# K of the last four-head step loaded in front of V of the step before it, and its TensorE scores moved

## The chip, the core and the metric

The kernel runs on one core of a Trainium2 chip. The core has a matrix engine (TensorE, PE in the profile; its weight loads are PEld), a vector engine (DVE), a scalar engine (ACT), GpSimd (POOL) and a queue engine (SP) that issues nearly all of the transfers here. Data comes from the chip's main memory into a memory of 128 partitions; matmul results go into a small accumulator memory (PSUM). The metric is device microseconds (us) of one execution; smaller is better.

## The reference

A decode step for a batch of B = 2: one token each, attention over a cache of 8,192 positions for 32 heads of 128, then a gated MLP. Nearly all of the bytes are the K and V caches, 2 x 32 x 8192 x 128 bf16 each.

```python
q = (x @ wq).reshape(B, Sq, Hq, Dh).transpose(0, 2, 1, 3)     # x is layernormed
scores = jnp.einsum("bhqd,bhkd->bhqk", q, k) * (Dh ** -0.5)
p = softmax(scores, axis=-1)
o = jnp.einsum("bhqk,bhkd->bhqd", p, v)
h = x + o.transpose(0, 2, 1, 3).reshape(B, Sq, Hq * Dh) @ wo
gate = layernorm(h) @ W_gate;  gate = gate * (gate > 0)
out = h + (gate * (layernorm(h) @ W_up)) @ W_down
```

## The kernel before

The 64 pairs of batch and head are done in 15 steps of four heads (steps 0 to 14; Q = LASTQ = 14) and two steps of two heads (15 and 16, called p0 and p1). K or V of a four-head step is 8 MB and fills one of three buffers of 128 partitions x 32,768 bf16 (`bufs`); K or V of a two-head step is 4 MB, half a buffer. Within a partition a buffer is a row of 256 tiles of 128 columns, one tile per group of cache positions.

For each step:

- `scores_pe` (L301) computes the scores of the last `npe` tiles of K on TensorE. In chunks of eight tiles, TensorE transposes them (L324), ACT copies the transposes back over the tiles (L325), and TensorE multiplies them with q (`times_q`, L315). The row that results is copied into the first eight of the now unused tiles (L333), transposed again (L337) and copied into the score column `scol` (L346). `npe` is 32; at the end 64 in step 14, 16 in step 15 and 32 in step 16 (`NPE_END`).
- `products` (L354) and `scores` (L365 to L373) compute the other `nv` tiles' scores on DVE: a product with q in place, four folds that halve the width, a sum into `scol`, and the maximum of each partition, `pm`.
- `largest` (L380) spreads the maxima by a matmul, and `exponentials` takes the minimum of their negatives (`nm`, L385) and has ACT write exp of the scores to `pgq` (four heads) or `pgp` (two heads), with their sums (L390).
- `values` (L403) multiplies the exponentials with V on TensorE, 64 matmuls for a four-head step, and ACT copies the result (L408); `diagonals` (L415) picks out each head's part.

The program order is written out by hand, and each engine takes its instructions in that order. All big loads stand on SP's queue. A load into a buffer waits for the last reader of the bytes that it overwrites, and a reader waits for the load that stands before it in program order and writes the bytes that it reads. In the loop over steps 0 to 13 (L477 to L497), V of the next step is loaded after `scores`, into the buffer that held K, and K of the step after next is loaded after `values`, into the buffer that held V. Step i has K in buffer 2i mod 3 and V in buffer (2i + 1) mod 3: K13 in 2, V13 in 0, K14 in 1, V14 in 2. K of steps 15 and 16 go to the halves of buffer 0, V of step 15 to the lower half of buffer 1 and V of step 16 to the lower half of buffer 2, in four pieces.

The weights of the second part follow in the free halves: `wo` in the upper half of buffer 1 (L506, L509: 16, 8 and 4 heads and the last four; the loads of 16, 8 and 4 heads start at columns 0, 8,192 and 12,288 of that half), W_gate and W_up in the upper half of buffer 2 (L544), W_down at the start of buffer 0 (L549). In program order the loads of V of step 15 and of `wo` stand behind `scores` of step 14 and in front of its `largest` and `exponentials`.

After step 14's exponentials, its values are done in eight groups of eight matmuls (`some_values`, L522), put between the TensorE scores of steps 15 and 16. Then come the values of step 15 (L559), DVE's `scores` of step 16 (L560), the output projection (`attend_set`, `attend`), the values of step 16 in column form (L426) and the MLP.

Of the kernel before, what the change touches and what calls it, by code (L numbers as in the profile page):

```python
# [23 lines left out]
def kernel(  # L24
# [14 lines left out]
    P = nc.NUM_PARTITIONS  # L39
    B, Sq, D = A_x.shape  # L40
    _, Hkv, Sk, Dh = A_k_cache.shape
    Hq = A_wq.shape[1] // Dh
    F = B_W_gate.shape[1]
    KC = D // P
# [3 lines left out]
    f32 = mybir.dt.float32  # L48
# [4 lines left out]
    LASTQ = B * NQ - 2  # L53
    TILE = NH * Sk * Dh // P
    HALF = TILE // 2
    TPC = 8
    VG = 4


    NPE = 32  # L60
    NPE_END = {LASTQ: 64, LASTQ + 1: 16, LASTQ + 2: 32}
    QZ = 64


    SETS = [(0, 16, 0), (16, 8, 16), (24, 4, 24)]
# [5 lines left out]
    FC = 11  # L71
# [44 lines left out]
    qrow = bufs[2][0:B, HALF:HALF + Hq * Dh]  # L116
    xr = bufs[2][0:B, HALF + Hq * Dh:HALF + Hq * Dh + D]

    wo = bufs[1][:, HALF:TILE]
    wgu = bufs[2][:, HALF:HALF + 2 * KC * F].rearrange("p (k c f) -> p k c f", k=2, c=KC)  # L120
    wd_sb = bufs[0][:, 0:FC * D].rearrange("p (c n) -> p c n", c=FC)


    class Step:
        def __init__(self, i):
            self.i = i
            self.quad = i <= LASTQ
            if self.quad:
                self.b, self.g = divmod(i, NQ)
                self.nh, self.nt = NH, TILE // Dh  # L130
                self.kt, self.vt = bufs[2 * i % 3], bufs[(2 * i + 1) % 3]
                self.qr = qrep[:, i, :]
                self.pg, self.zc = pgq, zc[:, self.b, self.g, :]
            else:
                k = i - LASTQ - 1
                self.b, self.g, self.k = B - 1, NQ - 1, k
                self.nh, self.nt = 2, HALF // Dh
                self.kt = bufs[0][:, k * HALF:(k + 1) * HALF]
                self.vt = bufs[1 + k][:, 0:HALF]
                self.qr = qpair[:, k, :]  # L140
                self.pg, self.zc = pgp[:, k], zc[:, self.b, self.g, 2 * k:2 * k + 2]
            self.npe = NPE_END.get(i, NPE)
            self.nv = self.nt - self.npe
            self.hp = P // self.nh
# [5 lines left out]
    Q = LASTQ  # L150

    def load_tile(cache, s, dst, pieces=1):
        h = NH * s.g + (0 if s.quad else 2 * s.k)
        n = s.nt * Dh
        w = n // pieces
        for k in range(pieces):
            nc.sync.dma_start(
                out=dst[:, k * w:(k + 1) * w], in_=_dram(cache, (s.b * Hkv + h) * Sk * Dh + k * w, [[n, P], [1, w]]),
            )
# [19 lines left out]
    with tc.manual_schedule():  # L179
# [105 lines left out]
        def sums(i):  # L285

            _, _, n, z = heads(i)
            z_ps[i] = ps.tile([P, n], f32, tag="mx", name="z_ps")
            nc.tensor.matmul(out=z_ps[i], lhsT=ones, rhs=z, start=True, stop=True)

        def shares(i):
            rzs[i] = small.tile([P, heads(i)[2]], f32, tag="rz", name="rz", bufs=2)
            nc.vector.reciprocal(out=rzs[i], in_=z_ps[i])

        def normalise(i):
            b, h0, n, _ = heads(i)
            nc.vector.tensor_tensor(out=ocol[:, h0:h0 + n, b], in0=o_ps[i][:, 0:n], in1=rzs[i], op=ALU.mult)

        scols = {}

        def scores_pe(s, between=lambda: None):  # L301


            U = s.npe // 4
            nh, nv = s.nh, s.nv
            row_ps = ps.tile([nh * U, 4 * P], f32, tag="row")

            def times_q(c0):
                for k in range(0, TPC, 4):
                    u = (c0 + k) // 4  # L310
                    if s.quad:
                        z = qz[:, QZ - NH - NH * u:QZ - NH - NH * u + NH * U]
                    else:
                        z = qzp[:, s.k, 14 - 2 * u:14 - 2 * u + 2 * U]
                    nc.tensor.matmul(  # L315
                        out=row_ps, lhsT=z, rhs=s.kt[:, (nv + c0 + k) * Dh:(nv + c0 + k + 4) * Dh],
                        start=(u == 0), stop=(u == U - 1),
                    )

            for c0 in range(0, s.npe, TPC):  # L320
                t_ps = ps2.tile([P, TPC, P], bf16, tag="tp")
                for k in range(TPC):
                    t = nv + c0 + k
                    nc.tensor.transpose(t_ps[:, k, :], s.kt[:, t * Dh:(t + 1) * Dh], ident)  # L324
                nc.scalar.activation(  # L325
                    out=s.kt[:, (nv + c0) * Dh:(nv + c0 + TPC) * Dh], in_=t_ps.rearrange("p t s -> p (t s)"), func=ACT.Copy,
                )
                between()
                if c0:
                    times_q(c0 - TPC)  # L330
            times_q(s.npe - TPC)
            rows = s.kt[0:nh * U, nv * Dh:nv * Dh + 8 * P].bitcast(f32)
            nc.scalar.activation(out=rows, in_=row_ps, func=ACT.Copy)  # L333
            between()
            sc_ps = ps.tile([P, 4, U, nh], f32, tag="row", name="sc_ps")
            for t in range(4):
                nc.tensor.transpose(  # L337
                    sc_ps[:, t].rearrange("p u j -> p (u j)"), rows[:, t * P:(t + 1) * P], ident_f[0:nh * U, 0:nh * U],
                )
            if s.i <= Q + 1:  # L340
                scols[s.i] = small.tile([P, TILE // Dh], f32, tag="scol", name="scol")[:, 0:s.nt]
            else:
                scols[s.i] = small.tile([P, s.nt], f32, tag="scolp", name="scolp")
            for j in range(nh):
                r = s.rows(j)
                nc.scalar.activation(  # L346
                    out=scols[s.i][r, nv:s.nt].rearrange("p (u t) -> p t u", t=4), in_=sc_ps[r, :, :, j], func=ACT.Copy,
                )

        def products(s, t0=0, t1=None):  # L350

            n = (s.nv if t1 is None else t1) - t0
            kv = _free(s.kt, t0 * Dh, [[Dh, n], [1, Dh]])
            nc.vector.tensor_tensor(out=kv, in0=kv, in1=_free(s.qr, 0, [[0, n], [1, Dh]]), op=ALU.mult)  # L354
# [42 lines left out]
        def values(s, u0, u1):  # L397

            r = slice(32 * (s.g % 4), 32 * (s.g % 4) + s.nh * VG)
            if u0 == 0:  # L400
                pv_ps[s.i] = ps2.tile([P, VG * Dh], f32, tag="o", name="pv_ps")
            for u in range(u0, u1):
                nc.tensor.matmul(  # L403
                    out=pv_ps[s.i][r, :], lhsT=s.pg[:, u].rearrange("p j t -> p (j t)"),
                    rhs=s.vt[:, u * VG * Dh:(u + 1) * VG * Dh], start=(u == 0), stop=(u == s.nt // VG - 1),
                )
            if u1 == s.nt // VG:
                nc.scalar.activation(out=pv[r, :], in_=pv_ps[s.i][r, :], func=ACT.Copy)  # L408
# [60 lines left out]
                )  # L469

        place_q(steps[0])
        def close(i):
            sums(i)
            shares(i)
            normalise(i)

        for i in range(Q):  # L477
            s = steps[i]
            scores_pe(s)
            place_q(steps[i + 1])  # L480
            products(s)
            scores(s)
            load_tile(A_v_cache, steps[i + 1], steps[i + 1].vt)
            largest(s)
            exponentials(s)
            if i - 1 in groups:
                close(i - 1)
            if i == 12:
                lay_rows(0, spread(0))
            values(s, 0, s.nt // VG)  # L490
            if i in groups:
                diagonals(i)
            if i + 2 <= Q:
                load_tile(A_k_cache, steps[i + 2], steps[i + 2].kt)
            else:
                for t in steps[Q + 1:]:
                    load_tile(A_k_cache, t, t.kt)  # L497


        s, p0, p1 = steps[Q:]  # L500
        scores_pe(s)
        products(s)
        scores(s)
        load_tile(A_v_cache, p0, p0.vt)
# [17 lines left out]
        def some_values():  # L522
            values(s, done[0], done[0] + 8)
            done[0] += 8
# [3 lines left out]
        load_tile(A_v_cache, p1, p1.vt, pieces=4)  # L528
        scores(p0)

        def values_or_largest():
            if done[0] < s.nt // VG:
                some_values()
            else:
                largest(p0)

        scores_pe(p1, values_or_largest)
        products(p1, 0, p1.nv // 2)
        exponentials(p0)
        sps = spread(1)  # L540
        products(p1, p1.nv // 2)
        for w, src, n in ((0, B_W_gate, 1), (1, B_W_up, KC // 2)):
            for c in range(0, KC, n):
                nc.sync.dma_start(  # L544
                    out=wgu[:, w, c:c + n], in_=_dram(src, c * P * F, [[F, P], [P * F, n], [1, F]]),
                )
# [89 lines left out]
        y = small.tile([P, B, KC], bf16, tag="y")  # L636
        nc.vector.tensor_tensor(out=y, in0=d_ps.rearrange("p c b -> p b c"), in1=hc, op=ALU.add)

        yrow = bufs[0][0:B * KC, HALF:HALF + P]
        yT_ps = ps2.tile([B * KC, P], bf16, tag="o")  # L640
        nc.tensor.transpose(yT_ps, y.rearrange("p b c -> p (b c)"), ident)
        nc.vector.tensor_copy(yrow, yT_ps)
# [31 lines left out]
```

## Time and profile before

| | |
|---|---|
| time, median of 3 runs | 662.42 us (662.28 to 664.31) |
| time of the profiled execution | 662.86 us |
| its span | 661.1 us |
| DVE busy | 527.8 us (80%) |
| PE busy | 386.1 us (58%) |
| ACT busy | 150.5 us (23%) |
| data moved by DMA | 281.44 MB, mean 426 GB/s |

The span is the stretch that the profiler covers; all times inside it count from its start. Busy shares are averages over the whole span. The strip of 40 slices on the page shows how they are spread, one slice being about 16.5 us, and the timeline lists single instructions with start, duration, engine, line, operation and what is written from what. For SP a row is the issue of a transfer; "us to landing" in the list of issues is from the issue until the data is there.

### The profile page before, as it was taken

The numbers are of one execution on the slowest core, as the hardware profiler recorded it, in microseconds if no ns is written. First come the engines' busy times: TensorE is split into PE (matmuls) and PEld (weight loads), VectorE is DVE, ScalarE is ACT, GpSimd is POOL, SyncE is SP. The second block draws the span as 40 slices with busy tenths as digits, with TensorE's granted clock in tenths as the row PEclk, the third lists the DMA queues.
The fourth block names the chain that finished last, engine by engine and source line by source line (L and its number), as shares of the span: only waits on it lengthen the run. The fifth ranks groups of instructions, "written<-read, shape, count | busy, mean of one in ns | idle before, by whom it ended". The sixth has DMA issues, their size and how long they took to land.

```text
span 661.1 us, 5492 instructions
## 1 busy us (share of the span) xinstructions
PE 386.1 (58%) x2347; PEld 179.1 (27%) x2347; DVE 527.8 (80%) x193; ACT 150.5 (23%) x323; POOL 5.2 (1%) x25
## 2 busy tenths in 40 slices
PE   3540854819276481927548192763909476397986
PEld 1120321304133240412214141221403233143446
DVE  2299696969969697996969789596988969698971
ACT  1130131311213132121312202131210313116420
POOL 2000000000000000000000000000000000000000
PEclk9875795959669595966959597695957869598985
DMA  9999989999999999999999999999999999999995
GB/s 381 445 440 444 444 386 444 437 441 444 432 406 444 433 436 440 429 420 444 437 424 434 436 436 433 444 417 440 440 417 436 440 429 436 433 408 434 421 417 223
DMA packets 8460, 281.44 MB, mean 426 GB/s; under 512 B 882, under 2 KB 2036, under 8 KB 3316
## 3 DMA queue, kind: packets, MB, share of 16 engines
q1 hardware_dynamic: 8432, 281.09, 98.7%
q8 instruction: 18, 0.29, 0.2%
q14 instruction: 6, 0.05, 0.0%
q10 hardware_dynamic: 4, 0.00, 0.0%
HBM read 281.09 MB, written 0.00 MB: 425 GB/s over the span
## 4 chain that ended last, share of the span: by engine, by line
DVE 35%; DMA 31%; PE 28%; ACT 4%; issue 1%; DVEq 0%; ACTq 0%
DMA tile<-in_A_k_cache_dram 29%; PE pv_ps L403 21%; DVE tile L354 16%; DVE tile L365 16%; ACT pgq L390 3%; DVE scol L369 2%; DMA tile<-in_A_wq_dram 2%; PE q_ps L240 1%; PE t_ps L324 1%; PE mx_ps L380 1%; PE row_ps L315 1%; PE o_ps L426 1%; DVE pm L373 1%; PE o_ps L415 0%; PE att_ps L459 0%
## 5 line engine op out<-in xcount | busy, mean ns | idle before, releaser
L354 DVE TENSOR_TENSOR tile<-tile,qrep 128x28672 bf16<-128x28672 bf16 (+1 forms) x15 | 224.3, 14950 | 73.5 <-DMA tile<-in_A_k_cache_dram 73.5
L403 PE MATMUL pv_ps<-tile,pgq 128*16 128x512 bf16 x960 | 245.3, 422 | 37.6 <-ACT pgq L390 37.6
L365 DVE TENSOR_TENSOR tile<-tile 128x14336 bf16<-128x14336 bf16 (+7 forms) x68 | 231.7, 3408 | 2.2
L403 PEld LDWEIGHTS <-pgq 128*16 128x16 bf16 x960 | 92.2, 98 | 184.1 <-issue 51.1
L380 PE MATMUL mx_ps<-nscale,pm 128*128 128x128 f32 x34 | 12.6, 470 | 175.0 <-DVE pm L373 175.0
L325 ACT ACTIVATE tile<-t_ps 128x1024 bf16<-128x1024 bf16 x70 | 70.0, 1023 | 30.7 <-PE t_ps L324 29.2
L390 ACT ACTIVATE pgq<-scol,nm 32x256 bf16<-32x256 f32 x60 | 30.3, 505 | 175.9 <-DVE nm L385 174.8
L408 ACT ACTIVATE pv<-pv_ps 16x512 f32<-16x512 f32 (+1 forms) x16 | 9.4, 589 | 239.1 <-PE pv_ps L403 238.3
L380 PEld LDWEIGHTS mx_ps<-nscale,pm 128*128 128x128 f32 x34 | 7.9, 290 | 177.6 <-DVE pm L373 176.7
L315 PE MATMUL row_ps<-tile,qz 128*32 128x512 bf16 (+1 forms) x128 | 38.8, 384 | 17.8 <-ACT tile L325 17.5
L324 PE MATMUL t_ps<-ident,tile 128*128 128x128 bf16 x560 | 42.6, 226 | 7.2 <-DMA tile<-in_A_k_cache_dram 7.2
L324 PEld LDWEIGHTS <-tile 128*128 128x128 bf16 x560 | 33.3, 101 | 29.2 <-issue 21.9
L369 DVE TENSOR_REDUCE scol<-tile 128x224 f32<-128x1792 bf16 (+2 forms) x16 | 31.1, 1944 | 1.6
L315 PEld LDWEIGHTS <-qz 128*32 128x32 bf16 (+1 forms) x128 | 10.8, 95 | 28.5 <-issue 21.8
L385 DVE TENSOR_REDUCE nm<-mx_ps 128x4 f32<-128x128 f32 (+1 forms) x17 | 5.0, 292 | 15.6 <-PE mx_ps L380 15.6
L346 ACT ACTIVATE scol<-sc_ps 32x32 f32<-32x32 f32 (+2 forms) x62 | 13.7, 222 | 10.3 <-PE sc_ps L337 9.2
L354 DVE TENSOR_TENSOR tile<-tile,qpair 128x6144 bf16<-128x6144 bf16 (+1 forms) x3 | 14.3, 4776 | 0.9 <-DMA tile<-in_A_k_cache_dram 0.9
L240 PE MATMUL q_ps<-tile,xn 128*2 128x512 bf16 x32 | 9.8, 471 | 8.3 <-DMA tile<-in_A_wq_dram 8.3
L243 DVE CAST tile<-q_ps 2x512 bf16<-2x512 f32 x8 | 5.4, 678 | 11.2 <-PE q_ps L240 11.2
L337 PE MATMUL sc_ps<-ident_f,tile 32*128 32x32 f32 (+3 forms) x68 | 7.3, 225 | 11.9 <-ACT tile L333 11.9
L333 ACT ACTIVATE tile<-row_ps 32x512 f32<-32x512 f32 (+3 forms) x17 | 10.0, 587 | 12.0 <-PE row_ps L315 12.0
L390 ACT ACTIVATION_READ_ACCUMULATOR pgq<-scol,nm 32x1 f32 x60 | 11.0, 184 | 0.0
(115 smaller groups left out, 114.2 us busy)
## 6 DMA issues: line engine op xcount, KB each, us to landing
tile<-in_A_k_cache_dram SPq DMA_DIRECT2D x2, 4096.0 KB, 26.1
tile<-in_A_wq_dram SPq DMA_DIRECT2D x1, 4096.0 KB, 12.1
tile<-in_A_v_cache_dram SPq DMA_DIRECT2D x1, 4096.0 KB, 21.6
tile<-in_A_v_cache_dram SPq DMA_DIRECT2D x4, 1024.0 KB, 21.1
tile<-in_A_wo_dram SPq DMA_DIRECT2D x1, 2048.0 KB, 26.1
tile<-in_B_W_gate_dram SPq DMA_DIRECT2D x4, 344.0 KB, 13.9
tile<-in_B_W_up_dram SPq DMA_DIRECT2D x2, 688.0 KB
tile<-in_A_wo_dram SPq DMA_DIRECT2D x1, 1024.0 KB, 28.0
```

The costliest lines, as they stand in the source:

```text
L240: nc.tensor.matmul(out=q_ps, lhsT=xn[:, c, :], rhs=wq_sb[:, c, n0:n0 + 4 * Dh], start=(c == 0), stop=(c == KC - 1),)
L315: nc.tensor.matmul(out=row_ps, lhsT=z, rhs=s.kt[:, (nv + c0 + k) * Dh:(nv + c0 + k + 4) * Dh], start=(u == 0), stop=(u == U - 1),)
L324: nc.tensor.transpose(t_ps[:, k, :], s.kt[:, t * Dh:(t + 1) * Dh], ident)
L325: nc.scalar.activation(out=s.kt[:, (nv + c0) * Dh:(nv + c0 + TPC) * Dh], in_=t_ps.rearrange("p t s -> p (t s)"), func=ACT.Copy,)
L333: nc.scalar.activation(out=rows, in_=row_ps, func=ACT.Copy)
L346: nc.scalar.activation(out=scols[s.i][r, nv:s.nt].rearrange("p (u t) -> p t u", t=4), in_=sc_ps[r, :, :, j], func=ACT.Copy,)
L354: nc.vector.tensor_tensor(out=kv, in0=kv, in1=_free(s.qr, 0, [[0, n], [1, Dh]]), op=ALU.mult)
L365: nc.vector.tensor_tensor(out=lo, in0=lo, in1=_free(s.kt, half, [[Dh, s.nv], [1, half]]), op=ALU.add)
L369: nc.vector.tensor_reduce(out=scol[:, 0:s.nv], in_=_free(s.kt, 0, [[Dh, s.nv], [1, 8]]), axis=AXIS.X, op=ALU.add,)
L380: nc.tensor.matmul(out=mx[s.i], lhsT=_free(pms[s.i], 0, [[0, P]]), rhs=nscale, start=True, stop=True)
L390: nc.scalar.activation(out=s.pg[r, :, j, :], in_=scol[r, :].rearrange("p (u t) -> p u t", t=VG), func=ACT.Exp, scale=SCALE, bias=nm[r, j:j ...
L403: nc.tensor.matmul(out=pv_ps[s.i][r, :], lhsT=s.pg[:, u].rearrange("p j t -> p (j t)"), rhs=s.vt[:, u * VG * Dh:(u + 1) * VG * Dh], start= ...
```

## The change

K of step 14 is loaded after `scores` of step 12, where V of step 13 was loaded, and V of step 13 after `values` of step 12, where K of step 14 was. To fit, K14 goes to buffer 0 and V13 to buffer 1, and what follows them changes places too: K of steps 15 and 16 and W_down go to buffer 1, V of step 15 and `wo` to buffer 0. The load of K of step 15 is put after the first half of step 13's values; the load of K of step 16 stays behind them.

`scores_pe` of step 14 is moved up from behind the loop into step 13, in front of its `largest`. Since the score column of step 13 is then still in use, the score columns of steps 14 to 16 get another place: inside the K buffer of the step itself, behind the eight tiles of the row (tiles nv + 8 and on, two bf16 columns for each f32 score).

Fewer tiles are scored on TensorE: 48 instead of 64 in step 14 and 16 instead of 32 in step 16, so DVE has 16 more in each. The last group of step 14's values comes behind step 16's `products` in program order, and `largest` of step 15 behind the seventh group instead of the last.

```diff
-    NPE_END = {LASTQ: 64, LASTQ + 1: 16, LASTQ + 2: 32}
-    QZ = 64
+    NPE_END = {LASTQ: 48, LASTQ + 1: 16, LASTQ + 2: 16}
+    QZ = 48
...
-    wo = bufs[1][:, HALF:TILE]
+    wo = bufs[0][:, HALF:TILE]
...
-    wd_sb = bufs[0][:, 0:FC * D].rearrange("p (c n) -> p c n", c=FC)
+    wd_sb = bufs[1][:, 0:FC * D].rearrange("p (c n) -> p c n", c=FC)
...
-                self.kt, self.vt = bufs[2 * i % 3], bufs[(2 * i + 1) % 3]
+                self.kt = bufs[0 if i == LASTQ else 2 * i % 3]
+                self.vt = bufs[1 if i == LASTQ - 1 else (2 * i + 1) % 3]
...
-                self.kt = bufs[0][:, k * HALF:(k + 1) * HALF]
-                self.vt = bufs[1 + k][:, 0:HALF]
+                self.kt = bufs[1][:, k * HALF:(k + 1) * HALF]
+                self.vt = bufs[2 * k][:, 0:HALF]
...
-            if s.i <= Q + 1:
-                scols[s.i] = small.tile([P, TILE // Dh], f32, tag="scol", name="scol")[:, 0:s.nt]
+            if s.i < Q:
+                scols[s.i] = small.tile([P, s.nt], f32, tag="scol", name="scol")
             else:
-                scols[s.i] = small.tile([P, s.nt], f32, tag="scolp", name="scolp")
+                scols[s.i] = s.kt[:, (nv + 8) * Dh:(nv + 8) * Dh + 2 * s.nt].bitcast(f32)
...
         for i in range(Q):
             s = steps[i]
             scores_pe(s)
             place_q(steps[i + 1])
             products(s)
             scores(s)
-            load_tile(A_v_cache, steps[i + 1], steps[i + 1].vt)
+            if i == Q - 2:
+                load_tile(A_k_cache, steps[Q], steps[Q].kt)
+            else:
+                load_tile(A_v_cache, steps[i + 1], steps[i + 1].vt)
+            if i == Q - 1:
+                scores_pe(steps[Q])
             largest(s)
             exponentials(s)
...
-            values(s, 0, s.nt // VG)
+            half = s.nt // VG // 2
+            values(s, 0, half)
+            if i == Q - 1:
+                load_tile(A_k_cache, steps[Q + 1], steps[Q + 1].kt)
+            values(s, half, 2 * half)
             if i in groups:
                 diagonals(i)
-            if i + 2 <= Q:
+            if i + 2 < Q:
                 load_tile(A_k_cache, steps[i + 2], steps[i + 2].kt)
+            elif i == Q - 2:
+                load_tile(A_v_cache, steps[Q - 1], steps[Q - 1].vt)
             else:
-                for t in steps[Q + 1:]:
-                    load_tile(A_k_cache, t, t.kt)
+                load_tile(A_k_cache, steps[Q + 2], steps[Q + 2].kt)
 
         s, p0, p1 = steps[Q:]
-        scores_pe(s)
         products(s)
         scores(s)
         load_tile(A_v_cache, p0, p0.vt)
...
-        def values_or_largest():
-            if done[0] < s.nt // VG:
-                some_values()
-            else:
+        def values_then_largest():
+            some_values()
+            if done[0] == s.nt // VG - 8:
                 largest(p0)
 
-        scores_pe(p1, values_or_largest)
+        scores_pe(p1, values_then_largest)
         products(p1, 0, p1.nv // 2)
         exponentials(p0)
         sps = spread(1)
         products(p1, p1.nv // 2)
+        some_values()
```

More of the change, by code (lines that the diff above doesn't have):

```diff
@@ L297, in normalise, with close @@
             nc.vector.tensor_tensor(out=ocol[:, h0:h0 + n, b], in0=o_ps[i][:, 0:n], in1=rzs[i], op=ALU.mult)
+        def close(i):
+            sums(i)
+            shares(i)
+            normalise(i)
         scols = {}
@@ L471 @@
         place_q(steps[0])
[L472 to L475, printed above, removed]
         for i in range(Q):
@@ L637 @@
         nc.vector.tensor_tensor(out=y, in0=d_ps.rearrange("p c b -> p b c"), in1=hc, op=ALU.add)
-        yrow = bufs[0][0:B * KC, HALF:HALF + P]
+        yrow = bufs[1][0:B * KC, HALF:HALF + P]
         yT_ps = ps2.tile([B * KC, P], bf16, tag="o")
```

## The prediction

> **What bounds the kernel now.** Times inside an execution are us from the start of the span. I read the page's strip of 40 slices first, then its list of DMA issues, then the timeline and the windows from 530 on, then the built program's order with what each instruction waits for.
>
> ```profile
> DVE  2299696969969697996969789596988969698971
> DMA  9999989999999999999999999999999999999995
> q1 hardware_dynamic: 8432, 281.09, 98.7%
> tile<-in_A_wo_dram SPq DMA_DIRECT2D x1, 2048.0 KB, 26.1
> tile<-in_A_wo_dram SPq DMA_DIRECT2D x1, 1024.0 KB, 28.0
> ```
>
> The transfers run from the first slice into the last; DVE, next at 80%, has pauses. All loads are on one queue. The reader should keep the last line: the 1 MB load of wo's eight heads takes 28.0 us from issue to landing, because others are in front of it. Now the timeline around the scores of step 14:
>
> ```profile
> 589.24 12.74 DVE L365 TENSOR_TENSOR tile<-tile 128x12288 bf16<-128x12288 bf16 x4
> 603.94 0.42 DVE L373 TENSOR_REDUCE pm<-scol 128x1 f32<-128x256 f32 x1
> 604.24 1.38 SPq L506 DMA_DIRECT2D tile<-in_A_wo_dram  x3
> 604.94 0.29 DVE L385 TENSOR_REDUCE nm<-mx_ps 128x4 f32<-128x128 f32 x1 [0.58 <-PE mx_ps L380]
> 605.33 0.51 ACT L390 ACTIVATE pgq<-scol,nm 32x256 bf16<-32x256 f32 x1 [1.42 <-DVE nm L385]
> 607.84 3.58 PE L403 MATMUL pv_ps<-tile,pgq 128*16 128x512 bf16 x8 [0.61 <-ACT pgq L390]
> 611.45 18.82 SPq L157 DMA_DIRECT2D tile<-in_A_v_cache_dram  x4
> ```
>
> wo's loads go out at 604.2 to 605.2, just ahead of the exponentials of step 14 (605.33), on which TensorE's values (607.84) wait. The load of eight heads, second of the three at L506, is issued at about 604.8 and lands at 604.8 + 28.0 = 632.8. The end of the kernel:
>
> ```profile
> 627.33 0.49 PE L380 MATMUL mx_ps<-nscale,pm 128*128 128x128 f32 x2
> 628.47 3.35 DVE L354 TENSOR_TENSOR tile<-tile,qpair 128x6144 bf16<-128x6144 bf16 x1
> 631.86 3.36 DVE L365 TENSOR_TENSOR tile<-tile 128x6144 bf16<-128x6144 bf16 x1
> 639.68 0.29 DVE L373 TENSOR_REDUCE pm<-scolp 128x1 f32<-128x128 f32 x1
> 640.79 0.49 PE L380 MATMUL mx_ps<-nscale,pm 128*128 128x128 f32 x2
> ```
>
> From the largest score of step 16 (640.79) to the end (661.1) one thing follows another, 20.3 us. The last W_down load, issued at 648.7, lands 7.3 us later, at 656.0; the output is written from 659.04.
>
> **What the program's order adds.** After the change the score column of step 14 (scol) lies in its own K buffer, buffer 0, at 128-column tiles nv + 8 = 216 to 220. wo now lies in the upper half of that buffer, and its eight-head load writes 4,096 columns from 16,384 + 16 x 512 = 24,576, which are tiles 192 to 224. In program order this load stands in front of the exponentials of step 14, as before. The built program shows the result: the first of these exponentials waits for that load's completion count, which it did not before, and the load waits for DVE's pm, the reduction that reads scol. So the exponentials of step 14 start when the load has landed (and take its bytes as the scores, which does not alter their time).
>
> **The change, part by part.**
>
> Exchange of K14 and V13. Both are 8 MB and take each other's place: K14 goes out at 531.1 (V13's time) and lands where V13 did, 531.1 + 25.8 = 556.9; V13 at 551.7 + 24.6 = 576.3. Values of step 13 began at 573.90 and now wait for V13 until 576.3, 2.4 later, and end at 592.1 instead of 589.74. The loads that this releases, K of 15 and of 16, go out at 585.3 and 592.1 while V14 is in transfer (to about 595.6, 19.3 us for 8 MB after 576.3), so the queue stays full: 0 on the transfers. Without that cover it would be 2.4.
>
> TensorE scores of step 14: 48 tiles instead of 64, so 16 transposes, 4 row products and 2 evictions of 1.02 less; what remains runs from 559 to about 569, after the scores of step 13. TensorE is idle there (0.00 busy in 560 to 570) and the next largest begins at 570.17. It costs nothing there; two evictions too late would be 2, still inside the 2.4 above.
>
> DVE, step 14: products no longer wait 4.96 for K14 and start at 571.3. With 208 tiles instead of 192: products 12.96 x 208/192 = 14.04, folds 12.74 x 208/192 = 13.80, reduction 1.75 to 1.90, pm 0.42, gaps 0.2. pm ends at 601.6 instead of 604.36. That is the gain of 2.7 that the reordering offers.
>
> wo's loads follow pm's release and go out at about 602 instead of 604.2, behind the same bytes (K15, K16, V15: 4 MB each, then 2 MB of wo). The queue being full, they land as before: the eight heads at 632.8. The bound from below is the shortest landing in the trace, 7.3 after issue (128 KB of W_down), so not before 609, which only rival 3 comes near; from above, the last piece of wo, issued 605.7 + 29.7 = 635.4. I take 632.8, the same load in the same place.
>
> The wait: exponentials of step 14 at 632.9 instead of 605.33. Behind them ACT holds the evictions for the TensorE scores of 15 and 16 and the later exponentials. TensorE holds the values of 14 and all after; SP holds the four pieces of V16 (issued from 611.45 before), gate and up, which need the values to free buffer 2. DVE does products and folds of 15 but its reduction waits for TensorE's row products, since their score column is in K too.
>
> From there, in TensorE order with the durations of before: exponentials 2.5, values start at 635.4 (607.84 before: +27.5). The stretch up to the score transposes of step 15 is unchanged (607.84 to 616.06), so 643.6. Then eight values 1.8, eight transposes 0.55, eight values 1.8, transposes 0.55, eight values 1.8, a last row product 0.2, eight values 1.8: 652.1. The largest of 15 follows, 0.49: 652.6. Before it ended at 627.82, 20.0 after the values began; now 17.2, since step 16 has two chunks of transposes fewer (with their values blocks moved behind).
>
> DVE then: nm 0.3, the two spreads 0.5, second products of step 16 (56 tiles: 3.35 x 56/48 = 3.91): 657.3. From there to pm of 16 the old rows took 639.97 - 631.74 = 8.23 for 96 tiles; with 112, folds (3.36 + 3.34) and reduction 0.95 grow by a sixth, 1.1, to 9.35: pm ends at 666.7. TensorE does the remaining values of 14 (654.8), and the 32 of step 15 from 657.8 in 6.9 to 8.7, done at 664.7 to 666.5. So DVE ends last, and the largest of 16 begins at 666.7 instead of 640.79: +25.9.
>
> Loads after the stall: V16's first piece goes out at 639.0; the remaining 8.2 MB at about 420 GB/s need 19.5, and with 2.4 of start (12.1 less 9.7 for 4 MB at rate) they land by 662. Their users come at 652 + 26 = 678 and later. Nothing on the path.
>
> The last 20.3: the same instructions; none waits for a load any more, at most 0.5 less. A lower clock there could cost up to 2, but 64 matmuls of L426 took 1.81 at a granted 0.55 to 0.59 and 64 of L459 1.74 near 1.00, so I take 0.
>
> Sum: 661.1 + 25.9 = 687.0 span. Around the span lie 662.86 - 661.1 = 1.76, so the profiled execution would be 688.8; it stood 0.44 above the median 662.42, which gives 688.4.
>
> **A rule against the row.** Landing at 632.8 rests on the queue's order: the last five landings before were V15 625.5, wo 630.3, 632.8, 634.0 and 635.4, in order of issue and spaced by size (2, 1, 0.5, 0.5 MB). The Trainium skill, DMA: Bandwidth & Descriptors, section Queues, rings and completion order, says that a DMA engine takes turns between the queue rows that have work, at packet granularity, and takes one ring's descriptors in order. All loads here share one row, so the trace agrees with its second half; turns between transfers would make the third rival below.
>
> **Rivals.**
>
> 1. The words of the change hold and the exponentials aren't held (not slower). They would start at 602.5, but the transposes of step 15 stand in front of the values on TensorE and need K15, which DVE and TensorE got at 606.2 before: values start 0.8 earlier, no more. DVE is equal until 631.8 and then has 16 tiles more in step 16, +1.1, so pm ends at 641.1 and the largest of 16 begins 0.3 later; the last landing stays at 656.0. Span 661.4, time 662.7. It decides if the exponentials begin by 605.3. For it: the 4.96 wait and the TensorE work of 591 to 603 do go away. Against it: the wait stands in the program, on a load that can't be issued before pm. 6 in 100.
>
> 2. Faster by over 0.3% (under 660.4): W_down would have to land 2 us before 656.0, with a queue at 98.7% and the same bytes. 2 in 100.
>
> 3. Transfers of the queue share the engines. Then the 1 MB load, issued at 602.6 with four others unfinished, lands after 5 x 1.05 MB at 430 GB/s = 12.2, near 615; values at 617.5, largest of 15 at 634.7 instead of 652.6, 18 less: 670. The 28.0 row speaks against it. 2 in 100.
>
> 4. The stall costs more: TensorE, idle for 29 us, stays at half clock (0.50 in 605 to 610, values 0.43 each against 0.21). The 48 values after the first eight would add 48 x 0.21 = 10: 698. Against it: clock 0.82 in 610 to 615 and 1.00 after, following a cold start as well. 4 in 100.
>
> **How the numbers follow.** The forecast has 86 in 100. Its own uncertainty is the landing (632 to 635.4), the clock of the end (0 to 2) and the DVE sums (1): 684 to 693. Outside are rivals 1 to 4 and a tail of the forecast, below 2 in 10. About 0.3% (2 us) is what a measurement of this kernel tells from no change. Slower: 86 + 2 + 4 = 92; same 6; faster 2.
>
> **What would show it.** Right: exponentials of step 14 idle for some 30 us until a wo load lands, near 632.9; ACT and TensorE empty from about 607 to 633; a slice or more of low GB/s around 635 to 641; K14 products starting at 571.3 without a DMA wait; pm of 14 near 601.6; largest of 16 near 666.7 and 20 us from there to the end. Wrong: exponentials near 602.5, or a landing of that load well before 630.

## The result and the profile after

The changed kernel takes 686.08 us (median of 6 runs, 685.62 to 687.46) against 663.06 for the kernel before beside it: ratio 1.0348, 95% interval 1.0332 to 1.0364, 23.0 us slower. The profiled execution took 686.07, its span is 684.2. In this kernel the exponentials of step 14 run after a load of wo has written over their score column, so they take bytes of wo in place of the scores of step 14, and its heads don't get the weights of the reference. The time is the subject here; the repair is in the first two experiments.

The page of the changed kernel, the rows that answer to those of before:

```profile
DVE  2298796969699796969699795969889799972381
DMA  9999999999999999999999999999999999999670
GB/s 387 461 437 429 429 426 429 427 433 437 430 430 433 445 433 434 437 433 426 429 442 437 433 430 433 434 433 433 442 433 429 430 423 433 420 432 402 231 276 3
q1 hardware_dynamic: 8432, 281.09, 95.5%
tile<-in_A_wo_dram SPq DMA_DIRECT2D x1, 1024.0 KB, 31.5
```

Up to slice 37 the queue is as full as before. A slice is now 17.1 us: the hole is in slices 38 and 39 (231 and 276 GB/s, from 633 on), and the last slice has hardly a transfer. The transfers did not get slower; they were stopped. The timeline of the changed kernel (start, duration, engine, line, operation; in brackets the idle time before and what ended it) shows where:

```profile
570.79 14.02 DVE L360 TENSOR_TENSOR tile<-tile,qrep 128x26624 bf16<-128x26624 bf16 x1
576.15 16.08 PE L409 MATMUL pv_ps<-tile,pgq 128*16 128x512 bf16 x64 [5.60 <-DMA tile<-in_A_v_cache_dram]
600.67 0.42 DVE L379 TENSOR_REDUCE pm<-tile 128x1 f32<-128x256 f32 x1
600.97 1.39 SPq L516 DMA_DIRECT2D tile<-in_A_wo_dram  x3
633.03 0.51 ACT L396 ACTIVATE pgq<-tile,nm 32x256 bf16<-32x256 f32 x1 [40.17 <-DMA tile<-in_A_wo_dram]
635.54 3.33 PE L409 MATMUL pv_ps<-tile,pgq 128*16 128x512 bf16 x8 [29.36 <-ACT pgq L396]
638.90 6.59 SPq L158 DMA_DIRECT2D tile<-in_A_v_cache_dram  x4
641.36 1.09 DVE L375 TENSOR_REDUCE tile<-tile 128x112 f32<-128x896 bf16 x1 [20.65 <-PE row_ps L321]
656.60 3.89 DVE L371 TENSOR_TENSOR tile<-tile 128x7168 bf16<-128x7168 bf16 x1
665.63 0.29 DVE L379 TENSOR_REDUCE pm<-tile 128x1 f32<-128x128 f32 x1
666.06 0.46 PE L386 MATMUL mx_ps<-nscale,pm 128*128 128x128 f32 x2 [2.15 <-DVE pm L379]
```

ACT is idle for 40.17 us before the first exponential of step 14 and is released by a load of wo. Some 10 us of that are no loss: the scores of step 14 are now done early, and ACT would be idle until about 602.7 in any case (second experiment). The hold is the other 30.3. The eight-head load went out at 601.4 and landed 31.5 later, at 632.9. Behind the exponential TensorE waits 29.36, DVE 20.65 (its reduction of step 15), and SP's four pieces of V16 leave at 638.9 instead of 611.45. The first two rows are the exchange: the products of step 14 no longer wait for K14, and the values of step 13 wait for V13. The windows (us busy and, in brackets, instructions of PE, PEld, DVE, ACT and POOL; then TensorE clock, DMA share, GB/s) give the same by stretch:

```profile
600.00:633.00 33.00, 2.39 (x12) 1.77 (x12) 16.72 (x10) 0.00 (x0) 0.00 (x0) 0.50 0.98 415
634.00:641.00 7.00, 5.46 (x28) 2.12 (x29) 0.00 (x0) 3.48 (x8) 0.00 (x0) 0.68 0.16 46
641.00:661.00 20.00, 18.84 (x114) 8.82 (x110) 14.10 (x11) 5.74 (x14) 0.00 (x0) 1.00 1.02 397
```

TensorE does 2.39 us of work in 33, ACT none, while the queue still runs. When ACT is let go, the queue has emptied, at 46 GB/s; from 641 on the released loads fill it again.

### The profile page after: what moved, and what is told of

Same layout as the page of the kernel before. It is cut to its first block, busy times and chain, and to the rows that moved or that the text cites. A ratio compares the mean times of both kernels' runs of the same rounds, so it can differ in the third digit from the quotient of the medians.

```text
span 684.2 us, 5411 instructions
## 1 busy us (share of the span) xinstructions
PE 377.6 (55%) x2307; PEld 176.1 (26%) x2307; DVE 532.0 (78%) x193; ACT 146.1 (21%) x319; POOL 5.1 (1%) x25
## 4 chain that ended last, share of the span: by engine, by line
DVE 39%; DMA 35%; PE 21%; ACT 2%; issue 1%; SPq 0%; DVEq 0%; ACTq 0%
DMA tile<-in_A_k_cache_dram 28%; DVE tile L360 18%; DVE tile L371 18%; PE pv_ps L409 16%; DMA tile<-in_A_wo_dram 5%; ACT pgq L396 2%; DVE scol L375 2%; DMA tile<-in_A_wq_dram 2%; PE q_ps L241 1%; PE mx_ps L386 1%; PE o_ps L432 1%; DVE pm L379 0%; DVE tile L375 0%; PE att_ps L465 0%; DVE nm L391 0%
## 5 line engine op out<-in xcount | busy, mean ns | idle before, releaser
L409 PE MATMUL pv_ps<-tile,pgq 128*16 128x512 bf16 x960 | 241.5, 418 | 69.0 <-ACT pgq L396 63.4
L371 DVE TENSOR_TENSOR tile<-tile 128x14336 bf16<-128x14336 bf16 (+5 forms) x68 | 233.7, 3437 | 2.2
L331 ACT ACTIVATE tile<-t_ps 128x1024 bf16<-128x1024 bf16 x66 | 65.9, 1022 | 27.2 <-PE t_ps L330 25.8
L321 PE MATMUL row_ps<-tile,qz 128*32 128x512 bf16 (+1 forms) x124 | 38.2, 390 | 18.4 <-ACT tile L331 18.1
L330 PE MATMUL t_ps<-ident,tile 128*128 128x128 bf16 x528 | 40.3, 227 | 9.4 <-DMA tile<-in_A_k_cache_dram 9.4
L375 DVE TENSOR_REDUCE scol<-tile 128x224 f32<-128x1792 bf16 x14 | 28.3, 2020 | 1.4
L375 DVE TENSOR_REDUCE tile<-tile 128x112 f32<-128x896 bf16 (+1 forms) x3 | 4.1, 1352 | 20.9 <-PE row_ps L321 20.7
L360 DVE TENSOR_TENSOR tile<-tile,qpair 128x7168 bf16<-128x7168 bf16 (+1 forms) x3 | 15.4, 5130 | 2.8 <-DMA tile<-in_A_k_cache_dram 2.8
L352 ACT ACTIVATE scol<-sc_ps 32x32 f32<-32x32 f32 x56 | 12.2, 218 | 8.3 <-PE sc_ps L343 7.3
L343 PE MATMUL sc_ps<-ident_f,tile 32*128 32x32 f32 (+2 forms) x68 | 7.3, 225 | 11.1 <-ACT tile L339 11.1
L339 ACT ACTIVATE tile<-row_ps 32x512 f32<-32x512 f32 (+2 forms) x17 | 10.0, 586 | 13.0 <-PE row_ps L321 13.0
## 6 DMA issues: line engine op xcount, KB each, us to landing
tile<-in_A_wo_dram SPq DMA_DIRECT2D x1, 1024.0 KB, 31.5
```

What stands on the lines that cost most here:

```text
L321: nc.tensor.matmul(out=row_ps, lhsT=z, rhs=s.kt[:, (nv + c0 + k) * Dh:(nv + c0 + k + 4) * Dh], start=(u == 0), stop=(u == U - 1),)
L331: nc.scalar.activation(out=s.kt[:, (nv + c0) * Dh:(nv + c0 + TPC) * Dh], in_=t_ps.rearrange("p t s -> p (t s)"), func=ACT.Copy,)
L352: nc.scalar.activation(out=scols[s.i][r, nv:s.nt].rearrange("p (u t) -> p t u", t=4), in_=sc_ps[r, :, :, j], func=ACT.Copy,)
L371: nc.vector.tensor_tensor(out=lo, in0=lo, in1=_free(s.kt, half, [[Dh, s.nv], [1, half]]), op=ALU.add)
L375: nc.vector.tensor_reduce(out=scol[:, 0:s.nv], in_=_free(s.kt, 0, [[Dh, s.nv], [1, 8]]), axis=AXIS.X, op=ALU.add,)
L409: nc.tensor.matmul(out=pv_ps[s.i][r, :], lhsT=s.pg[:, u].rearrange("p j t -> p (j t)"), rhs=s.vt[:, u * VG * Dh:(u + 1) * VG * Dh], start= ...
```

## The experiments

Each run is compared with the kernel before on the same chip.

**Does taking the wait away give the 23 us back?** Two ways, so that neither's side effect decides. In the first the score column of step 14 leaves the K buffer, and its exponentials read the scores again:

```diff
-    ones = consts.tile([P, P], f32)
+    ones = consts.tile([P, 1], f32)
...
-            nc.tensor.matmul(out=z_ps[i], lhsT=ones, rhs=z, start=True, stop=True)
+            nc.tensor.matmul(out=z_ps[i], lhsT=_free(ones, 0, [[0, P]]), rhs=z, start=True, stop=True)
...
+            elif s.i == Q:
+                scols[s.i] = small.tile([P, s.nt], f32, tag="scolq", name="scolq")
...
```

> The changed kernel, but the score column of step 14 has a place of its own outside the K buffer, so no load of wo writes over it; to make room the tile of ones is one column, read with a step of zero. Theory (the wait on the wo load is the whole loss): exponentials of step 14 at about 602.5 instead of 633.0, values from about 607, time 662.7 (661 to 664.5), within 0.3% of before. Rival (the exchange of K14 and V13, the moved scores or DVE's 16 + 16 more tiles cost a part of the 23): the time stays above 665, by that part.

Measured: 662.39 us, ratio 0.9989 (0.9979 to 0.9998); the first exponential of step 14 starts at 602.26. In the second the column stays and the loads move:

```diff
+        largest(s)
+        exponentials(s)
         for k, (h0, n, at) in enumerate(SETS):
...
-        largest(s)
-        exponentials(s)
```

> The changed kernel with the score column where it is, but the four loads of wo behind the exponentials of step 14 in program order. Theory: the exponentials wait for DVE alone and start at about 602.5; the eight-head load waits for them instead, goes out at about 605 and lands at 633 as before, since the queue is full; time 662.7 (661 to 664.5), same as e1_own_column within 1 us. Rival (the place inside the K buffer itself costs, by waits of DVE or ACT on neighbouring bytes): slower than e1_own_column by more than 1.5 us.

Measured: 662.55 us, ratio 0.9982 (0.9970 to 0.9993). The timeline of this second kernel:

```profile
600.96 0.42 DVE L379 TENSOR_REDUCE pm<-tile 128x1 f32<-128x256 f32 x1
601.26 4.74 SPq L518 DMA_DIRECT2D tile<-in_A_wo_dram  x3
602.71 0.51 ACT L396 ACTIVATE pgq<-tile,nm 32x256 bf16<-32x256 f32 x1 [8.78 <-DVE nm L391]
605.61 7.62 DVE L360 TENSOR_TENSOR tile<-tile,qpair 128x14336 bf16<-128x14336 bf16 x1 [2.99 <-DMA tile<-in_A_k_cache_dram]
```

The exponential starts at 602.71, released by nm. The three loads now take SP 4.74 instead of 1.39, because the second waits for the exponentials; it costs nothing, as the queue in front of it is full. Both kernels lie within 0.2 us of each other. So the place inside the K buffer costs nothing by itself that these two runs could tell, and everything else in the change together is a gain of 0.1 to 0.2%: the rivals of both runs fall.

**Does the overlap alone, in the kernel before, make the loss?** Nothing exchanged, nothing moved; the exponentials of step 14 read the load's bytes:

```diff
-            if s.i <= Q + 1:
+            if s.i == Q:
+                scols[s.i] = s.kt[:, (nv + 8) * Dh:(nv + 8) * Dh + 2 * s.nt].bitcast(f32)
+            elif s.i <= Q + 1:
```

> The kernel before with one edit: the score column of step 14 lies inside its K buffer (tiles 200 to 204 of buffer 1), where the eight-head load of wo, which stands ahead in program order, writes; its exponentials read that load's bytes, as in the changed kernel. Nothing is exchanged or moved. Theory: exponentials at 632.9 instead of 605.3, largest of step 16 near 667.7, 18.1 to 20.3 from there to the end, time 686 to 690 (+23 to +27). Rival (the loss needs the exchange or the new order of TensorE's work): 663, no change.

Measured: 688.90 us, ratio 1.0387 (1.0369 to 1.0405), 25.3 us more than 663.64 beside it. Its timeline:

```profile
632.23 0.51 ACT L392 ACTIVATE pgq<-tile,nm 32x256 bf16<-32x256 f32 x1 [27.95 <-DMA tile<-in_A_wo_dram]
668.27 0.49 PE L382 MATMUL mx_ps<-nscale,pm 128*128 128x128 f32 x2
```

The releaser is the same load, and the exponential starts 0.8 us earlier than in the changed kernel; the largest of step 16 starts 0.6 us later than expected. The overlap is sufficient by itself.

**Does the time follow that one landing?** The eight-head load is put ahead of V of step 15; the exponentials still read its bytes:

```diff
+        h0, n, at = SETS[1]
+        nc.sync.dma_start(
+            out=wo[:, at * D:(at + n) * D], in_=_dram(A_wo, h0 * Dh * D, [[n * D, P], [1, n * D]]),
+        )
         load_tile(A_v_cache, p0, p0.vt)
-        for k, (h0, n, at) in enumerate(SETS):
+        for k, (h0, n, at) in enumerate(SETS[::2]):
```

> The changed kernel, with the eight-head load of wo issued ahead of V of step 15 instead of behind it and the sixteen-head load; the exponentials still read that load's bytes. Theory (the time follows that landing one to one): it lands 6 MB, 14.6 us, earlier, near 618.3 instead of 633.0, and the time is 686.1 - 14.6 = 671.5 (669.5 to 673.5). Rival (the stall is of another load, or of the queue as a whole): 686. A landing that moves while the time follows by less than half would mean that another chain takes over from there.

Measured: 671.52 us, ratio 1.0122 (1.0107 to 1.0137). The load landed at 617.7 (issued 601.5, 16.2 later):

```profile
617.74 0.51 ACT L396 ACTIVATE pgq<-tile,nm 32x256 bf16<-32x256 f32 x1 [24.37 <-DMA tile<-in_A_wo_dram]
651.78 0.46 PE L386 MATMUL mx_ps<-nscale,pm 128*128 128x128 f32 x2 [0.49 <-DVE pm L379]
```

The exponential is 15.3 earlier than in the changed kernel, the largest of step 16 14.3 earlier, the time 14.6 shorter. One to one within a microsecond; no other chain takes over down to this point. It also shows that the wait is for one load's place in the queue, not for the queue to drain.

**What is the rest of the change worth?** As the second experiment, with the old TensorE shares:

```diff
-    NPE_END = {LASTQ: 48, LASTQ + 1: 16, LASTQ + 2: 16}
-    QZ = 48
+    NPE_END = {LASTQ: 64, LASTQ + 1: 16, LASTQ + 2: 32}
+    QZ = 64
...
-            some_values()
-            if done[0] == s.nt // VG - 8:
+            if done[0] < s.nt // VG:
+                some_values()
+            else:
                 largest(p0)
...
-        some_values()
```

> As e2_loads_behind, but with the old TensorE shares (64, 16 and 32 tiles in steps 14, 15 and 16) and the old places of the last value group and of the largest of step 15; what stays of the change is the exchange of K14 and V13 and the scores of step 14 moved up. Theory: 662.2 (660.5 to 664): the last landing (near 656.0) sets the end, so the 1.1 us that DVE saves in step 16 against e2_loads_behind comes out as 0 to 1. Rival (DVE's 16 more tiles are the bound at the end): faster than e2_loads_behind by 1.2 us or more.

Measured: 661.45 us, ratio 0.9974 (0.9963 to 0.9986). It is 1.1 us under the second experiment by the medians, 0.5 by the ratios (0.0008 of 663), and the two intervals overlap: between theory and rival, so the times don't settle how much the DVE tiles cost. In the profiled executions, one of each kernel, the largest of step 16 begins at 639.31 here and at 640.93 in the second experiment, and the spans differ by the same 1.6 (659.6 and 661.2). In both, TensorE comes to it straight from the values of step 15, with pm done 0.7 and 0.6 before. Those values start 0.6 earlier here, because TensorE doesn't wait 1.74 for a reciprocal behind DVE's longer product, and they run 1.0 shorter (8.74 against 9.75). The trace of this run shows no wait for a load of W_down. So the theory's reason, that the last landing sets the end, isn't borne out, and the rival's DVE tiles act through TensorE's start; why the values run shorter wasn't tried. It is the fastest kernel of the study, 0.26% under the one before, which is less than the 0.3% named in the prediction.

## Why the prediction was right

The exchange: products of step 14 start at 570.79 (forecast 571.3), values of 13 at 576.15 (576.3), pm of 14 ends at 601.1 (601.6). Each of these moved as worked out, within 0.5, and the transfers stayed full up to 633.

The wait: landing at 632.9 (632.8), first exponential 633.03 (632.9), values from 635.54 (635.4), largest of 15 done at 652.0 (652.6), pm of 16 at 665.9 (666.7), largest of 16 at 666.06 (666.7). From 640.79 this is +25.3; the prediction had 25.9. The last transfer, issued at 655.5, landed 7.8 later, at 663.3 (662), nowhere on the path. The prediction had 8.2 MB of loads behind the stall. The list of issues adds up to 8,256 KB (V16 4,096, gate and up 1,376 each, W_down 1,408), which is 8.45 MB at 1,024 bytes a KB, so at its 420 GB/s 20.1 us and not 19.5.

One term came out by luck. Folds and reduction of step 16, 7.65 in all, were to grow "by a sixth, 1.1"; a sixth of 7.65 is 1.28. They measured 8.79 (3.89, 3.81 and 1.09), 1.14 more, so the slip lay nearer than the sum meant.

The step that was mis-sized is the last one, "the last 20.3: the same instructions ... at most 0.5 less". It measured 684.2 - 666.06 = 18.1, and 25.3 - 2.2 gives the 23.1 by which the spans differ. (The 0.44 that the prediction took off at the end, because the profiled execution stood above the median, did not come again: 686.07 against 686.08.) Two pieces make up the 2.2. In the kernel before, ACT's copy of step 15's values ended late (the first three rows), so the output projection began 1.66 after the largest (640.79 to 642.45); after the change it began 1.11 later (667.17), since the copy was done before it (the last three rows):

```profile
640.79 0.49 PE L380 MATMUL mx_ps<-nscale,pm 128*128 128x128 f32 x2
640.89 0.59 ACT L408 ACTIVATE pv<-pv_ps 8x512 f32<-8x512 f32 x1 [8.50 <-PE pv_ps L403]
642.45 1.74 PE L459 MATMUL att_ps<-orow,tile 128*128 128x2 bf16 x64
```

```profile
663.96 0.59 ACT L414 ACTIVATE pv<-pv_ps 8x512 f32<-8x512 f32 x1 [6.82 <-PE pv_ps L409]
666.06 0.46 PE L386 MATMUL mx_ps<-nscale,pm 128*128 128x128 f32 x2 [2.15 <-DVE pm L379]
667.17 1.74 PE L465 MATMUL att_ps<-orow,tile 128*128 128x2 bf16 x64
```

And a pause of 1.56 in step 16's values is gone:

```profile
647.61 0.19 PE L426 MATMUL o_ps<-pgp,tile 128*128 128x2 bf16 x2
649.37 1.79 PE L426 MATMUL o_ps<-pgp,tile 128*128 128x2 bf16 x62 [1.56 <-issue]
```

That is the kernel before; the same group in the changed one:

```profile
672.43 1.84 PE L432 MATMUL o_ps<-pgp,tile 128*128 128x2 bf16 x64
```

The third experiment parts the two: there the output projection begins 1.67 after the largest, as before, only the pause is missing, and the end takes 18.7 (687.0 - 668.27), 1.6 less than 20.3.

Rival 1 is what the first two experiments ran: it gave 0.3 us more than before, they measured 0.7 to 0.8 less by the medians, both within 0.3%. The forecast that the reordering's 2.7 us of earlier scores would come to nothing held: K15 in the second experiment landed at 605.6, 2.99 after DVE was free. Rival 3 falls by the fourth experiment, where the load's place in the queue set its landing. Rival 4 falls by the clock, 1.00 from 641 to 661, where all but the first sixteen values of step 14 run, eight of them in 1.89. Rival 2 did not come about: even the kernels without the wait have medians above 660.4.

The Trainium skill, DMA: Bandwidth & Descriptors, section Queues, rings and completion order, has a ring's descriptors taken in order; the landings of the fourth experiment agree (617.7 when ahead of V15, 632.9 when behind it).

## What to carry to other kernels

Putting a small buffer into the free part of a big one is only free while the next load into that part stands behind the last reader in program order. If the load stands ahead of the reader, the order that keeps races out turns it into a wait for everything queued in front of that load, here 31.5 us from issue to landing for 1 MB, and the reader gets the new bytes. After such a move, look in the built program's waits for a load's completion that the reader did not wait for before. In a trace the sign is a reader that is released by a load whose data it has no use for.

## What the runs showed that was not expected

The 1.3 to 1.6 us pause of TensorE in step 16's values, which the profile puts down to "issue", is there in all four kernels in which the queue is still full at that time (409 GB/s at 647 to 650 in the kernel before; first, second and last experiment 1.30, 1.35 and 1.45). It is missing in the three in which the queue is empty there (at most 8 GB/s: the changed kernel, the overlap alone, the eight-head load ahead of V15). The traces hold a hint. In each of the four, a 16 KB transfer of the instruction queue (q8 on the page) starts 0.8 to 1.0 us before the pause, and TensorE goes on 1.2 to 1.3 us after it has ended: in the kernel before it runs from 647.0 to 648.0, the pause from 647.8 to 649.4. In the three others that transfer is over before the group of matmuls begins (in the changed kernel 670.1 to 671.2, the group at 672.43). So TensorE may have waited for its own instructions, held up by the full queue; that is a coincidence in time in seven traces, and no run tried it.
